# Fewer, larger groups of small attention matmuls between the large products of a fused attention and feed-forward kernel

## The chip, the cores and the metric

One core of a Trainium2 chip runs the kernel. The metric is the device time of one execution in microseconds, lower being better. The core has five engines with queues of their own that run in program order: TensorE (PE) multiplies matrices into PSUM, VectorE (DVE) and ScalarE (ACT) compute on tiles and empty PSUM, GpSimd (POOL) computes a little and issues loads, SyncE (SP) issues stores and DMA transposes. [...]

## The reference

Attention works on chunks of 64 tokens, each by itself, for 8 batches, 8 heads, 576 tokens (9 chunks) and a head dimension of 64. Its output, as 4608 rows of 512, goes through a feed-forward network with a SiLU whose slope differs for each hidden unit.

```python
scores = scale * np.matmul(q_c, k_c.transpose(0, 1, 2, 4, 3))   # per chunk of 64
scores = scores - np.max(scores, axis=-1, keepdims=True)
attn = np.exp(scores)
attn = attn / (np.sum(attn, axis=-1, keepdims=True) + 1e-09)
out = np.matmul(attn, v_c)
x = np.ascontiguousarray(out.transpose(0, 2, 1, 3)).reshape(B * S, H * D)
h = x @ w_in                                    # 4608x512 by 512x2048
g = h * (1.0 / (1.0 + np.exp(-beta * h)))
return (g @ w_out).astype(np.float32)           # 2048x512
```

## The kernel before, in words

The 4608 rows are nine blocks (NB) of 512 rows. A block is 8 chunks, taken from the flat order of batches and chunks. The whole order of instructions is written out by hand; each engine runs its own in that order. While block j goes through the feed-forward layers, the attention of block j+1 (`na`) and the scores of block j+2 are made between its matmuls.

**Attention.** `emit_T` (L136) transposes a part of q or k on DVE; a batch has four such parts, taken with `T(b)`. `emit_sc(g)` makes the scores of a group of four chunks: 64 matmuls with 32 contraction rows each (L164) into two banks, and two Exps on ACT (L173) into the tiles et. `emit_pv(i)` takes two chunks: 16 matmuls of 64 rows (L192) multiply et by v with a column of ones, so that the row sums come out beside the result. DVE takes the reciprocal of the sums (L207, or L204 when the two halves lie in separate tiles) and multiplies (L209) into x16. Then either a DMA transpose on SP's queue (L217), or in block 0 and for block 1 `emit_xp` (four PE transposes, L226, and a copy by ACT, L229), gives the block's input xt. One block needs two groups of scores and four PVs.

**First layer.** Block 0 and block 1 use plain matmuls (`L1_plain`; `emit_h` L252, SiLU by `emit_g` L262). From block 2 on, `L1` computes half of the hidden units by a scheme of seven products instead of eight: `unit` 0 and 1, whose `prod` (L305) adds into a bank A (tag sc0 or sc1) and two more, B and C (tag x). DVE copies partial results out: u1 before A is added to again, then u2, u3 and w1 (L313), and combines them to c1 (L327, L340). The other half of the hidden units is plain; three `spacers` for each unit place those matmuls between the products. The SiLUs of a unit are at L316. `emit_xs` (L285 to L288), four subtractions on DVE, makes inputs of these products from xt before the layer begins.

**Second layer.** Block 0 uses `L2_plain` (L504): 16 pieces of four matmuls, each with a hook for attention before it. Its weights are first divided by beta (`scale_w_out`: L123 on ACT, L127 on DVE). From block 1 on, `steps_L2` gives seven products mm0 to mm6 of 16 matmuls each (`prod`, L405), whose terms s1 to s4 are sums and differences of activations (`emit_sum`, L363 to L369, in four parts each). mm0 fills bank A, mm1 B, mm2 A again, mm3 D, mm4 A, mm5 C and mm6 A. ACT copies A out between (u1, u2, u3; L416), and `cB`, `cD`, `cC` combine the banks on DVE (L424). `fill` and `dve(n)` place pending s1 and s2 subtractions. The order in which a product runs through its eight parts is KO = (0, 1, 4, 5, 2, 3, 6, 7).

**Banks.** The pool ps_p has four banks for hidden units and second-layer products; ps_s has one each under the tags sc0 and sc1; ps_x has one tile of two banks, tag x. In the kernel before, scores use sc0 and sc1 and a PV uses x, except for the opening, where `spare` puts some of them in ps_p. A tile that is allocated again waits until its last reader is done.

**Around block j's second layer** the order in the queues of blocks 2 to 7 is: mm0, PV 0, mm1, PV 1, cB, mm2, PV 2, mm3, PV 3, load of the Exp table, scores of the first group, four s4 subtractions, mm4, cD, mm5, cC, scores of the second group, xs of the next block, mm6, load of the SiLU table (`table`, L653). In block 1 the scores lie a little otherwise, since the transposes of q and k come later there. Transposes for a later batch lie in the spacers 10, 13, 14 and 15 of the first layer.

Of the kernel before, what the change touches and what calls it, by code (L numbers as in the profile page):

```python
# [8 lines left out]
FP32 = mybir.dt.float32  # L9
# [6 lines left out]
def kernel(  # L16
# [103 lines left out]
    def scale_w_out(g, act=False):  # L120
        for kk in range(4 * g, 4 * g + 4):
            if act:
                nc.scalar.activation(  # L123
                    out=wo(kk), in_=wo(kk), func=ACTF.Copy,
                    scale=binv[:, kk % 2, kk // 2:kk // 2 + 1])
                continue
            nc.vector.tensor_scalar_mul(wo(kk), wo(kk), binv[:, kk % 2, kk // 2:kk // 2 + 1])  # L127
# [20 lines left out]
    def emit_sc(g, spare=False, between=None):  # L148
        sc = [
            ps_p.tile([128, 2, 4, CH], FP32, tag="p", name=f"scp{s}") if spare  # L150
            else ps_s.tile([128, 2, 4, CH], FP32, tag=f"sc{s}", name=f"sc{s}")
            for s in range(2)
        ]
        for z in range(2):
            if z and between:
                between()
            for c in range(4):
                b, cb = divmod(4 * g + c, NCB)
                for e in range(2):
                    for a in range(4):  # L160
                        p0, o0 = 32 * a, 64 * (a // 2)
                        kk = kT[b][p0:p0 + 32, z].rearrange("p t r e -> p (t r) e")
                        qq = qT[b][p0:p0 + 32, z].rearrange("p t r e -> p (t r) e")
                        nc.tensor.matmul(  # L164
                            out=sc[a % 2][o0:o0 + 64, z, c, :],
                            lhsT=kk[:, cb * CH:(cb + 1) * CH, e],
                            rhs=qq[:, cb * CH:(cb + 1) * CH, e],
                            start=(e == 0),
                            stop=(e == 1),
                        )  # L170
        for s in range(2):
            et = et_p.tile([128, 2, 4, CH], FP16, tag=f"et{s}", name=f"et{s}")
            nc.scalar.activation(out=et, in_=sc[s], func=ACTF.Exp, scale=scale)  # L173
            et_t[g, s] = et
# [5 lines left out]
    def emit_pv(i, spare=False, xbar=True):  # L180
        g = i // 2
        if spare:
            xs = [ps_p.tile([128, 4, 128], FP32, tag="p", name="xp") for _ in range(2)]
        else:
            x = ps_x.tile([128, 2, 4, 128], FP32, tag="x", name="x")
            xs = [x[:, 0], x[:, 1]]
        for s in range(4):
            z, a2 = s // 2, s % 2
            for hp, cp in ((0, 0), (1, 1), (0, 1), (1, 0)):
# [4 lines left out]
                    lhsT=et_t[g, a2][p0:p0 + 64, z, 2 * (i % 2) + cp, :],  # L194
# [193 lines left out]
    def steps_L2(j, last=False):  # L388
# [11 lines left out]
        def prod(name, a, b, first, rows=(0, 1)):  # L400
            if first and name not in bank:
                grab(name)
            for i in rows:
                for n, kk in enumerate(KO):
# [24 lines left out]
        def mm0():  # L429
            grab("B")  # L430
            prod("A", g[:, 0:NM, up], b11, True)
            take("u1", "A")
# [141 lines left out]

    with tc.manual_schedule():
# [25 lines left out]
        for f in T_items(0):  # L601
# [13 lines left out]
        emit_sc(1, spare=True)  # L615
        emit_idle(3)
        emit_pv(0, xbar=False)
        emit_pv(1, spare=True, xbar=False)
# [5 lines left out]
        emit_pv(3, spare=True, xbar=False)  # L624
# [10 lines left out]
        scale_w_out(2, act=True)  # L635
        T1[2]()
        T1[3]()
        scale_w_out(3)
# [3 lines left out]
            9: lambda: emit_sc(2),  # L642
            12: lambda: [emit_pv(4, xbar=False), emit_sc(3)],
            13: lambda: [emit_pv(5, xbar=False), emit_xp(4)],
            14: lambda: [emit_pv(6, xbar=False), emit_xp(5)],
            15: lambda: [emit_pv(7, xbar=False), emit_xp(6)],
# [5 lines left out]
        def table(func):  # L652
            nc.scalar.activation(out=warm2, in_=warm, func=func, scale=1.0)  # L653

        table(ACTF.Silu)
        TQ = {b: T_items(b) for b in range(2, B)}

        def T(b, n=1):
            for _ in range(n):
                if TQ.get(b):  # L660
                    TQ[b].pop(0)()
# [9 lines left out]
        for j in range(1, NB):  # L671
            na = j + 1
            late = j == 1
            if late:
                L1_plain(1, {
                    -1: lambda: emit_xp(7), 3: lambda: emit_tw(3), 4: lambda: T(2), 5: lambda: T(2),
# [3 lines left out]
                    KFF: lambda: [table(ACTF.Exp), emit_sc(4)],  # L680
                }, 2)
            else:
                L1(j, {8: lambda: loads(j), 10: lambda: T(j + 2), 11: lambda: loads_v(j), 13: lambda: T(j + 2),
                       14: lambda: T(j + 2), 15: lambda: T(j + 2)})

            def pv(n):
                if na < NB:
                    emit_pv(4 * na + n)

            def sc(n):  # L690
                if na + 1 < NB:
                    emit_sc(2 * na + 2 + n)
# [4 lines left out]
            emit_sum(j, 3, 3)  # L697
            if late:
                dve(8)
                T(3)  # L700
            pv(0)
            dve(4)
            mm[1]()
            if late:
                T(3)
                emit_sc(5)
            pv(1)
            cB()
            dve(2)
            mm[2]()  # L710
            pv(2)
            dve(2)
            mm[3]()
            pv(3)
            if not late:
                table(ACTF.Exp)
                sc(0)
# [4 lines left out]
            if late:  # L722
                sc(0)
# [3 lines left out]
            sc(1)  # L727
# [3 lines left out]
            table(ACTF.Silu)  # L731
# [30 lines left out]
```

## Time and profile before

| What | Value |
|---|---|
| Median of 8 runs | 282.54 us (282.29 to 283.3) |
| Profiled execution, whole | 282.52 us |
| Its span in the trace | 280.7 us |
| Granted TensorE clock | 1.0 |
| Second layer of block 0 begins on PE | 33.6 us |
| Second layer of block 1 begins on PE | 66.9 us |
| First layer of blocks 2, 3, 4 begins on PE | 83.5, 111.8, 140.1 us |
| Score matmuls, busy (x1088) | 12.5 us |
| PV matmuls into x, busy (x544) | 11.3 us |

A block in the steady part takes 28.3 us. In a timeline line the first number is the start in us from the span's start, the second the length of the merged stretch, then engine, line, operation, output and inputs, the shape and the count; in brackets stands the idle time of the engine ahead of it and who ended it. The ends of matmuls are modelled and overlap the next ones, so the distance between starts is what a matmul costs in PE's queue. Page lines on busy time give the sum, the share of the span and the number of instructions.

### The profile page before, as it was taken

To read this page: it belongs to the slowest core of one execution; us is meant where nothing else is said; L and a number is where in the kernel's file an instruction comes from. 1 tells how busy PE (TensorE), PEld (TensorE's weight loads), DVE (VectorE), ACT (ScalarE), POOL (GpSimd) and SP (SyncE) were. 2 spreads that over 40 slices of the span, in tenths; PEclk is the share of its full clock that TensorE was granted. 3 is DMA by queue.
4 is the path that set the end of the run, shared out by engine and by line. 5 is a ranking of instruction groups with operands and counts; after the bars stand their busy time and mean duration, and the time that the engine had idled before them with its cause. 6 is when DMAs were issued, how large, how long until landed. Compare 5 with 4: busy or idle time off the path is not lost.

```text
span 280.7 us, 8175 instructions
## 1 busy us (share of the span) xinstructions
PE 266.4 (95%) x3509; PEld 187.4 (67%) x3509; DVE 209.2 (75%) x395; ACT 170.7 (61%) x291; POOL 99.3 (35%) x108
## 2 busy tenths in 40 slices
PE   2679999899999999999999999999999999999995
PEld 0355445545886678667866786688668866876684
DVE  2772645897668997799778987898659865986684
ACT  2249736778247844785478547854785478527842
POOL 8743252171107710781068104810342034203400
PEclk9999999999999999999999999999999999999999
DMA  6999999999737933794479342924201420142013
GB/s 104 172 206 211 211 181 205 223 216 185 108 72 155 171 73 86 156 171 59 101 144 175 56 109 75 84 41 118 75 0 40 117 75 0 40 114 75 5 37 112
DMA packets 69588, 31.99 MB, mean 114 GB/s; under 512 B 53680, under 2 KB 63920, under 8 KB 69552
## 3 DMA queue, kind: packets, MB, share of 16 engines
q0 software_dynamic: 44960, 18.35, 54.1%
q1 hardware_dynamic: 24448, 12.99, 17.3%
q8 instruction: 27, 0.44, 0.7%
q10 hardware_dynamic: 144, 0.13, 0.1%
q14 instruction: 9, 0.07, 0.1%
HBM read 36.71 MB, written 9.44 MB: 164 GB/s over the span
## 4 chain that ended last, share of the span: by engine, by line
PE 79%; DVE 8%; ACT 5%; DMA 3%; issue 2%; POOL 2%; ACTq 0%; DVEq 0%; POOLq 0%
PE hps L252 22%; PE oA L405 18%; PE wA L305 7%; PE wX L305 6%; PE oB L405 5%; PE oD L405 5%; PE ops L504 4%; PE oC L405 4%; PE sc L164 3%; DMA vb<-in_v_dram 3%; PE x L192 3%; ACT gt L316 2%; DVE kT L136 2%; ACT L653 1%; DVE x L209 1%
## 5 line engine op out<-in xcount | busy, mean ns | idle before, releaser
L252 PE MATMUL hps<-xt,wi 128*128 128x512 f16 (+1 forms) x376 | 85.3, 365 | 1.0 <-ACT xt L229 0.9
L262 ACT ACTIVATE gt<-hps,beta 128x512 f16<-128x512 f32 x88 | 57.8, 682 | 19.4 <-PE hps L252 19.4
L252 PEld LDWEIGHTS <-wi 128*128 128x128 f16 x376 | 36.7, 98 | 30.2 <-issue 1.5
L405 PEld LDWEIGHTS <-s 128*128 128x128 f16 x496 | 46.7, 98 | 6.6 <-DVE s L369 0.5
L405 PE MATMUL oA<-tw,s 128*128 128x256 f16 x368 | 44.1, 273 | 0.0
L405 PEld LDWEIGHTS <-gt 128*128 128x128 f16 x384 | 35.7, 98 | 7.8 <-ACT gt L316 1.8
L173 ACT ACTIVATE et<-sc 128x512 f16<-128x512 f32 x34 | 18.4, 594 | 29.2 <-PE sc L164 29.2
L416 ACT COPY u<-oA 128x512 f32<-128x512 f32 x24 | 14.0, 585 | 33.9 <-PE oA L405 33.9
L313 DVE COPY u<-wA 128x512 f32<-128x512 f32 x42 | 28.6, 682 | 4.8 <-PE wA L305 4.8
L99 POOL DMA_DIRECT2D vb<-in_v_dram x32 | 27.4, 876 | 9.4 <-DMA wi<-in_moe_w_in_dram 5.5
L336 POOL TENSOR_TENSOR t<-u,w 128x512 f32<-128x512 f32 x14 | 17.8, 1273 | 34.4 <-DVE u L313 34.4
L474 POOL TENSOR_TENSOR o<-t,o 128x512 f32<-128x512 f32 x7 | 8.9, 1268 | 53.4 <-ACT o L471 53.4
L305 PEld LDWEIGHTS <-sw 128*128 128x128 f16 x224 | 21.9, 98 | 8.5
L443 POOL TENSOR_TENSOR w<-u,u 128x512 f32<-128x512 f32 x7 | 8.8, 1264 | 45.1 <-ACT u L416 45.1
L209 DVE TENSOR_TENSOR x<-x,rd 128x512 f16<-128x512 f32 x34 | 23.5, 691 | 1.2
L653 ACT ACT_TABLE_LOAD x17 | 21.8, 1283 | 4.1 <-DVE oe L485 3.8
L136 DVE STREAM_TRANSPOSE qT<-qu 128x576 f32<-128x576 f32 x16 | 19.9, 1242 | 4.5 <-DMA qu<-in_q_dram 4.5
L367 POOL TENSOR_TENSOR s<-gt 128x512 f16<-128x512 f16 x16 | 18.2, 1154 | 11.9 <-ACT gt L262 11.9
L136 DVE STREAM_TRANSPOSE kT<-ku 128x576 f32<-128x576 f32 x16 | 19.9, 1244 | 3.0 <-DMA ku<-in_k_dram 3.0
L305 PEld LDWEIGHTS <-wi 128*128 128x128 f16 x168 | 16.4, 98 | 4.9
L316 ACT ACTIVATE gt<-c,beta 128x512 f16<-128x512 f32 x28 | 18.7, 716 | 0.2
L164 PE MATMUL sc<-qT,kT 32*64 32x64 f16 x1088 | 12.5, 194 | 6.2 <-DVE kT L136 5.6
(86 smaller groups left out, 389.0 us busy)
## 6 DMA issues: line engine op xcount, KB each, us to landing
out_dram<-osb SPq DMA_DIRECT2D x21, 256.0 KB, 2.8
vb<-in_v_dram POOLq DMA_DIRECT2D x32, 144.0 KB, 7.4
qu<-in_q_dram POOLq DMA_DIRECT2D x7, 576.0 KB, 7.0
ku<-in_k_dram POOLq DMA_DIRECT2D x7, 576.0 KB, 9.1
out_dram<-o SPq DMA_DIRECT2D x14, 256.0 KB, 2.2
wi<-in_moe_w_in_dram POOLq DMA_DIRECT2D x4, 512.0 KB, 12.0
w_out<-in_moe_w_out_dram POOLq DMA_DIRECT2D x4, 512.0 KB, 16.1
qu<-in_q_dram POOLq DMA_DIRECT2D x2, 288.0 KB, 5.4
```

What stands on the lines that cost most here:

```text
L99: nc.gpsimd.dma_start(out=t[64 * hp:64 * hp + 64, 2 * z:2 * z + 2, :, 0:D].rearrange("p s c d -> p (s c) d"), in_=v[b, h0:h0 + 2].rearrang ...
L136: nc.vector.transpose(out=dst[b][:, z].rearrange("p t r e -> p (t r e)").bitcast(FP32).rearrange("p (t r) -> p r t", r=RUN), in_=src[b][:, ...
L164: nc.tensor.matmul(out=sc[a % 2][o0:o0 + 64, z, c, :], lhsT=kk[:, cb * CH:(cb + 1) * CH, e], rhs=qq[:, cb * CH:(cb + 1) * CH, e], start=(e ...
L173: nc.scalar.activation(out=et, in_=sc[s], func=ACTF.Exp, scale=scale)
L209: nc.vector.tensor_tensor(out=yy, in0=src, in1=rr.to_broadcast(shape), op=ALU.mult,)
L252: nc.tensor.matmul(out=hps_t[j, m][:, c0:c1], lhsT=w_r[m // 4][:, 2 * z + e, m // 2 % 2, m % 2, :], rhs=xt_t[j][:, n, c0:c1], start=(n == ...
L262: nc.scalar.activation(out=gt_t[j][:, m, :], in_=hps, func=ACTF.Silu, scale=beta2[:, m % 2, m // 2:m // 2 + 1],)
L305: nc.tensor.matmul(out=bank[b][:, i, :], lhsT=a[:, kk, q, i, :], rhs=rhs[:, kk, :], start=(first and i == 0 and kk == 0), stop=(kk == 1), ...
L313: nc.vector.tensor_copy(out=sb[nm], in_=bank[b])
L316: nc.scalar.activation(out=gt_t[j][:, m, cols], in_=src, func=ACTF.Silu, scale=beta2[:, m % 2, m // 2:m // 2 + 1],)
L405: nc.tensor.matmul(out=bank[name][:, i, :], lhsT=a[:, kk, i * 128:(i + 1) * 128], rhs=b[:, kk, :], start=(first and i == 0 and n == 0), st ...
L653: nc.scalar.activation(out=warm2, in_=warm, func=func, scale=1.0)
```

## The change

The attention of a block in blocks 2 to 6 stands in three places instead of five: PV 0 and 1 together after mm1, PV 2 and 3 together after mm3, and both groups of scores together after mm4. The second PV of a pair uses the banks sc0 and sc1 and is evacuated in two halves; the first group of scores uses the tile x and gets one Exp of 1024 columns instead of two of 512. et becomes one tile for both halves. All pending s1 and s2 subtractions come ahead of the first PV. In block 1, both groups of scores 4 and 5 stand ahead of mm0, and the rest as in the later blocks. Block 7 has only the PVs and block 8 has no attention.

In block 0, the second layer has the scores of groups 2 and 3 together before piece 8, PV 4 and 5 before piece 10, PV 6 and two transposed inputs before 12, PV 7 and one before 14. The last two quarters of w_out are each scaled half by ACT and half by DVE, the last quarter later than before. The Exp table is loaded before them, and the SiLU table after the last transposed input of block 1 instead of ahead of it.

mm0 runs through its parts in the order 0, 1, 4, 5, 6, 7, 2, 3. The transpose of q or k that stood in spacer 15 of the first layer comes ahead of its first product (`first`), after xs in DVE's queue. The Exp table's load moves from after mm3 and PV 3 to ahead of PV 2, and it and the SiLU table's are left out where no scores follow.

```diff
-    def scale_w_out(g, act=False):
-        for kk in range(4 * g, 4 * g + 4):
-            if act:
+    def scale_w_out(g, act=0):
+        for n, kk in enumerate(range(4 * g, 4 * g + 4)):
+            if n < act:
...
-    def emit_sc(g, spare=False, between=None):
...
+    def emit_sc(g, where="s", between=None):
+        if where == "x":
+            scx = ps_x.tile([128, 2, 2, 4, CH], FP32, tag="x", name="scx")
+            sc = [scx[:, 0], scx[:, 1]]
...
-        for s in range(2):
-            et = et_p.tile([128, 2, 4, CH], FP16, tag=f"et{s}", name=f"et{s}")
-            nc.scalar.activation(out=et, in_=sc[s], func=ACTF.Exp, scale=scale)
-            et_t[g, s] = et
+        et = et_t[g] = et_p.tile([128, 2, 2, 4, CH], FP16, tag="et", name="et")
+        for o, i_ in [(et, scx)] if where == "x" else [(et[:, s], sc[s]) for s in range(2)]:
+            nc.scalar.activation(out=o, in_=i_, func=ACTF.Exp, scale=scale)
...
+        elif where == "s":
+            xs = [ps_s.tile([128, 4, 128], FP32, tag=f"sc{h}", name="xp") for h in range(2)]
...
-            prod("A", g[:, 0:NM, up], b11, True)
+            prod("A", g[:, 0:NM, up], b11, True, order=(0, 1, 4, 5, 6, 7, 2, 3))
...
         T1[0]()
         T1[1]()
-        scale_w_out(2, act=True)
         T1[2]()
         T1[3]()
-        scale_w_out(3)
+        scale_w_out(2, act=2)
+        table(ACTF.Exp)
         load_v(2)
         load_qk(3)
         hooks = {
-            9: lambda: emit_sc(2),
-            12: lambda: [emit_pv(4, xbar=False), emit_sc(3)],
-            13: lambda: [emit_pv(5, xbar=False), emit_xp(4)],
-            14: lambda: [emit_pv(6, xbar=False), emit_xp(5)],
-            15: lambda: [emit_pv(7, xbar=False), emit_xp(6)],
+            8: lambda: [emit_sc(2, "x"), emit_sc(3)],
+            10: lambda: [emit_pv(4, xbar=False), emit_pv(5, "s", xbar=False), scale_w_out(3, act=2)],
+            12: lambda: [emit_pv(6, xbar=False), emit_xp(4), emit_xp(5)],
+            14: lambda: [emit_pv(7, xbar=False), emit_xp(6)],
         }
...
-        table(ACTF.Silu)
...
-                    -1: lambda: emit_xp(7), 3: lambda: emit_tw(3), 4: lambda: T(2), 5: lambda: T(2),
+                    -1: lambda: [emit_xp(7), table(ACTF.Silu)], 3: lambda: emit_tw(3), 4: lambda: T(2), 5: lambda: T(2),
...
-                    KFF: lambda: [table(ACTF.Exp), emit_sc(4)],
+                    KFF: lambda: [table(ACTF.Exp), emit_sc(4, "x"), emit_sc(5)],
...
-                L1(j, {8: lambda: loads(j), 10: lambda: T(j + 2), 11: lambda: loads_v(j), 13: lambda: T(j + 2),
-                       14: lambda: T(j + 2), 15: lambda: T(j + 2)})
...
+                L1(j, {8: lambda: loads(j), 10: lambda: T(j + 2), 11: lambda: loads_v(j),
+                       13: lambda: T(j + 2), 14: lambda: T(j + 2)}, first=lambda: T(j + 2))
...
             mm[0]()
             emit_sum(j, 3, 1)
             emit_sum(j, 3, 3)
+            dve(8)
             if late:
-                dve(8)
-                T(3)
-            pv(0)
-            dve(4)
+                T(3, 2)
             mm[1]()
-            if late:
-                T(3)
-                emit_sc(5)
-            pv(1)
+            pv(0, "x")
+            pv(1, "s")
             cB()
-            dve(2)
             mm[2]()
-            pv(2)
-            dve(2)
             mm[3]()
-            pv(3)
-            if not late:
+            if na + 1 < NB and not late:
                 table(ACTF.Exp)
-                sc(0)
+            pv(2, "x")
+            pv(3, "s")
             for p in range(4):
                 emit_sum(j, 4, p)
             mm[4]()
             cD()
-            if late:
-                sc(0)
+            if na + 1 < NB:
+                emit_sc(2 * na + 2, "x")
+                emit_sc(2 * na + 3)
             mm[5]()
             if j < NB - 1:
                 cC()
-            sc(1)
             if na < NB:
                 emit_xs(na)
             mm[6]()
-            table(ACTF.Silu)
+            if na + 1 < NB:
+                table(ACTF.Silu)
```

## The prediction, made before the result

> **What bounds the kernel now.** I read the page first, then the chain that ended last, then PE's timeline of one whole block beside DVE's and ACT's.
>
> ```profile
> PE 266.4 (95%) x3509; PEld 187.4 (67%) x3509; DVE 209.2 (75%) x395; ACT 170.7 (61%) x291; POOL 99.3 (35%) x108
> PE 79%; DVE 8%; ACT 5%; DMA 3%; issue 2%; POOL 2%; ACTq 0%; DVEq 0%; POOLq 0%
> ```
>
> PE is busy 95% of the span and holds 79% of the chain: it sets the end, and only what shortens or stops its queue counts. PE's timeline of block 3 (start, duration), then the oC stall in block 7:
>
> ```profile
> 124.79 2.15 PE L405 MATMUL oA<-w_out,gt 128*128 128x256 f16 x16
> 126.86 0.32 PE L192 MATMUL x<-vb,et 64*64 64x65 f16 x16
> 127.11 1.92 PE L405 MATMUL oB<-w_out,gt 128*128 128x256 f16 x16
> ...
> 129.22 1.92 PE L405 MATMUL oA<-tw,s 128*128 128x256 f16 x16
> 131.07 0.32 PE L192 MATMUL x<-vb,et 64*64 64x65 f16 x16
> 131.32 1.92 PE L405 MATMUL oD<-tw,gt 128*128 128x256 f16 x16
> 133.17 0.32 PE L192 MATMUL x<-vb,et 64*64 64x65 f16 x16
> 133.42 0.71 PE L164 MATMUL sc<-qT,kT 32*64 32x64 f16 x64
> 134.06 1.92 PE L405 MATMUL oA<-tw,s 128*128 128x256 f16 x16
> 135.82 1.91 PE L405 MATMUL oC<-w_out,s 128*128 128x256 f16 x16
> 137.66 0.71 PE L164 MATMUL sc<-qT,kT 32*64 32x64 f16 x64
> 138.30 1.92 PE L405 MATMUL oA<-tw,s 128*128 128x256 f16 x16
> ...
> 248.60 1.70 PE L405 MATMUL oC<-w_out,s 128*128 128x256 f16 x14 [0.25 <-DVE s L369]
> ```
>
> Starts, not durations, give the cost in PE's queue. A product followed by a product takes 134.06 to 135.82, 1.76; between undisturbed ones it is 1.75. Hence a PV group costs 129.22-127.11-1.75 = 0.36, PV with a score half 134.06-131.32-1.75 = 0.99, a lone score half 138.30-135.82-1.75 = 0.73. A block pays 3x0.36+0.99+0.73 = 2.80 for its five groups. Each group's time is largely the change of shape: PV's 16 starts span 0.13, and the rest is the step in (0.09) and out (0.12).
>
> The opening already has two such groups side by side:
>
> ```profile
> 12.12 0.45 PE L164 MATMUL sc<-qT,kT 32*64 32x64 f16 x32 [0.52 <-DVE bt L603]
> 12.40 0.75 PE L164 MATMUL scp<-qT,kT 32*64 32x64 f16 x64
> 15.13 0.25 PE L192 MATMUL x<-vb,et 64*64 64x65 f16 x7 [1.02 <-DMA vb<-in_v_dram]
> 15.20 0.32 PE L192 MATMUL xp<-vb,et 64*64 64x65 f16 x16
> 15.45 0.39 PE L235 MATMUL idle<-zero 128*128 128x256 f16 x2
> ```
>
> The second PV begins 0.07 after the rest of the first and is out at 15.45: 0.25 with the step out, so 0.13 joined. The joined score half is 12.40 to 13.08 less 0.12 out, 0.56.
>
> DVE where the next block's first layer begins (140.06 on PE):
>
> ```profile
> 137.84 0.69 DVE L424 TENSOR_TENSOR t<-oC,w 128x512 f32<-128x512 f32 x1 [0.51 <-PE oC L405]
> 139.57 0.42 DVE L288 TENSOR_TENSOR xs<-xt,xs 128x512 f16<-128x512 f16 x1
> 140.70 0.69 DVE L313 COPY u<-wA 128x512 f32<-128x512 f32 x1 [0.71 <-PE wA L305]
> 144.94 1.25 DVE L136 STREAM_TRANSPOSE qT<-qu 128x576 f32<-128x576 f32 x1
> 146.03 0.68 DVE L340 TENSOR_TENSOR c<-wX,u 128x512 f32<-128x512 f32 x1
> ```
>
> DVE is idle 0.71 before the copy u1; PE's third product (141.79) overwrites the bank that u1 reads, and u1 is out at 141.39: 0.40 to spare. A transpose holds DVE for 1.09 (144.94 to 146.03).
>
> **What the Trainium skill says.** TensorEngine Tiling (Array Packing), Key Properties: changing the tiling mode drains TensorE, changing only the tile does not. The trace agrees: 0.12 from a PV group to a product or to a score group, none between the two PVs at 15.20. TensorE: Matmul & The Clock Gate, Back-to-back issue gap: N/2.4+2.5 ns, 109 at 256 columns; the trace has 109. The same page, Architectural detail: ACT and DVE queues are strict FIFO; that is why an item moved ahead of u1 delays u1. ScalarE: Activation LUTs, What ACT_TABLE_LOAD costs: 1283 ns (the trace: 1283), and 186 ns + 0.833 per element without pointer operands; my estimate of the new 1024-wide Exp from this is 1.04, against 1.09 for today's pair.
>
> **The change part by part.**
>
> *Groups, blocks 2 to 6.* Two PV pairs at 0.36+0.13 and a score pair at 0.73+0.56: 0.98+1.29 = 2.27 for 2.80, so -0.53 a block. Cover: PV pair 2 needs the banks of pair 1. DVE takes a split PV in two halves of 0.55 (16.28 to 16.83), 1.09 for 0.84, +0.50 a block. From the start E of oA: all sums now stand ahead of the first evacuation; the last silu of t ends at E+1.5 (126.30), so sums end near E+5.1, evacuations at E+7.05, cB at E+7.65; pair 2 can be evacuated from about E+8.1. The score pair waits for the second half of pair 2, ready at E+10.1, wanted at E+10.5. s4 part 2 is there about 0.25 before its matmul in mm5. No wait, but thin.
>
> *Kk order of mm0.* Today the sixth matmul waits 0.22 for gt 3 (silu ends 125.50). Moved to the eighth place it doesn't wait. But mm1 follows directly now: its eighth matmul (gt 15) falls at E+2.51, and that silu ends at 127.45, E+2.66, plus 0.06. So the 0.22 goes and 0.21 comes back in oB: -0.01.
>
> *A transpose moved from the end of L1 to its front (blocks 2 to 5).* It stands between xs and u1. Let F be the end of oC's slot (137.57). DVE: t at F+0.27, four xs, the transpose at F+2.37, u1 from F+3.47 to F+4.15. In the kernel before PE's third product stood at F+4.22, since a lone score group lay in between. That group is gone from there: mm6 ends at F+1.75, the third product is due at F+1.75+1.73 = F+3.48. PE waits 0.72 with the semaphore. The later steps move with it and DVE recovers by the next spacer. +0.72 in four blocks; leaving the end of L1 wins nothing, since the silus gate the sums. Blocks 6 to 8 have no transposes left.
>
> *Block 7.* No scores: PV pairs save 4x0.36-2x0.49 = 0.46. But without a score pair mm5 comes right after mm4, while pair 2's evacuations (1.94) and the four s4 subtractions (0.33 each) follow each other on DVE. First s4 0.62 late, part 2 1.06 late, where 0.41 is lost today: +0.65. Net +0.17, with -0.02 for mm0.
>
> *Block 0, second layer.* Groups on PE's timeline, each less the 0.216 of a 512-column step: a score group 0.74, PV with scores 1.06 (44.82 to 45.79 and the step in), three PVs with PE transposes of 0.58, and a wait of 0.25 for an x16: 3.79. New: score pair 1.29, PV pair 0.49, PV with two transposes 0.80, PV with one 0.58: 3.16, so -0.63. The scaling of w_out's last quarter, halved, stays covered: ACT's two take 0.64 each behind the landing at 44.16 and are due at 46.6; DVE's two fit between evacuations, before 47.0. Then this:
>
> ```profile
> 51.17 1.28 ACT L653 ACT_TABLE_LOAD   x1
> 52.57 0.57 ACT L229 COPY xt<-xps 128x512 f16<-128x512 f16 x1
> ```
>
> PE waits 0.85 more than its own step, until 53.19, for this copy behind the table load. The load moves behind it; about 0.3 of copy latency stays: -0.55. Together -1.18: hps would resume at 52.0. The silus start 0.9 late and catch up within four banks.
>
> *Block 1.* 53.19 to 83.48 is 30.29 today. New: L1 13.05, seven products 12.23, two score pairs 2.58, two PV pairs 0.98: 28.84. -1.45. The first score pair's Exps end at 69.4 and u1's copy at 69.9, before the PVs (69.9) and mm2 (70.4): tight.
>
> *Rest.* SP still issues four transposes, but the third and fourth are back to back (1.2 each); the fourth lands about 3.3 after issue, 5.7 after pair 2 against xs at 6.0. The last table load (1.28) ran beside the last store: -0.05.
>
> Sum: -1.18-1.45+4x(0.72-0.53-0.01)-0.55+0.17-0.05 = -2.34. The profiled execution took 282.52 (span 280.7), the median is 282.54: 280.2.
>
> **Unknown costs.** The wait on u1: 0 (if DVE's queue were ahead by more than I read) to 0.9; I take 0.72. Joined PV: 0.13 to 0.36 (no join). Block 0: 0.5 to 1.4 gained. Block 1: 1.0 to 1.5. Nothing on PE can gain beyond the groups and waits named: the large matmuls keep their step of 0.109 throughout.
>
> **Rivals.**
> A, the sum: 280.2; its own range 279.4 to 281.2. Chance 0.52.
> B, the moved transpose is hidden after all: 282.54-2.34-2.88 = 277.3. For it: DVE idles 0.71 there now. Against: F+4.15 versus F+3.48. 0.15.
> C, opening and block 1 give half: waits on Exps, u1 or DMA take 1.3: 281.5. 0.13.
> D, slower: the fourth DMA transpose lands late, holding xs, the moved transpose and u1 in blocks 2 to 5. One issue of 134.78 lasted 2.11; two such back to back plus landing come to 6.8 after pair 2, 0.8 late: +3.4, 283.6. It decides for slower from 0.7 late. For it: DVE gives it later; against: most issues last 1.20. 0.13.
> E, the pairs don't join: fourteen pairs lose 0.23, 283.4. Against: 15.20. 0.07.
>
> A measurement tells 0.2% (0.57) from nothing. Faster: A, B and 0.08 of C, 0.75; same: 0.05 of C, 0.03 of D, 0.02 of E, 0.10; slower 0.15. Range 278.2 to 282.2.
>
> **What will show it.** Right: PE's third product wA in blocks 2 to 5 waits about 0.7 on DVE's u1 and not in 6 to 8; block period from 28.28 to about 28.46, block 6 at 27.56; oB waiting 0.2 on gt; oC in block 7 waiting about 1.1; hps resuming near 52.0. Wrong: an xs waiting on DMA, scores waiting on DVE, or a period under 28.0.

## The result: slower, by waits that are not in the groups

| | before | changed |
|---|---|---|
| Median of the runs compared | 282.79 us (282.29 to 284.7, 32 runs) | 289.0 us (284.54 to 290.61, 11 runs) |
| Ratio changed to before | | 1.0126 [1.0096, 1.0156] |
| Profiled execution, its span | 282.52, 280.7 | 285.13, 283.4 |

The kernel got slower, and its executions now spread over 6 us, where before all lay within 2.4 and most within 1. The ratio leaves out the executions that lie more than 1.5% above the kernel's fastest, here six of twelve (289.0 and up); they are the upper end of its own spread, so the loss between the two medians, 2.2%, is larger. The profiled execution is one of the quick ones; a later profile of the same kernel, of an execution of 288.14, stands at the end of the experiments.

The two lines of the page on busy time and on the chain that ended last:

```profile
PE 264.2 (93%) x3509; PEld 187.4 (66%) x3509; DVE 213.8 (75%) x425; ACT 163.5 (58%) x276; POOL 100.6 (36%) x108
PE 72%; DVE 11%; DMA 11%; POOL 2%; issue 2%; ACT 1%; DVEq 0%; ACTq 0%; POOLq 0%
```

PE has 2.2 us less to do (264.2 for 266.4), as it should. But the chain has left PE: 72% for 79%, while DMA went from 3% to 11% and DVE from 8% to 11%. So look for PE waiting on DVE, and DVE on a transfer.

First the groups. PE's timeline of block 2's second layer (start, length, the merged stretch):

```profile
98.62 0.32 PE L198 MATMUL x<-vb,et 64*64 64x65 f16 x16
98.77 0.30 PE L198 MATMUL xp<-vb,et 64*64 64x65 f16 x16
99.00 1.92 PE L411 MATMUL oA<-tw,s 128*128 128x256 f16 x16
100.76 1.91 PE L411 MATMUL oD<-tw,gt 128*128 128x256 f16 x16
102.60 0.32 PE L198 MATMUL x<-vb,et 64*64 64x65 f16 x16
102.75 0.30 PE L198 MATMUL xp<-vb,et 64*64 64x65 f16 x16
102.98 1.92 PE L411 MATMUL oA<-tw,s 128*128 128x256 f16 x16
104.83 0.71 PE L168 MATMUL scx<-qT,kT 32*64 32x64 f16 x64
105.36 0.86 PE L168 MATMUL sc<-qT,kT 32*64 32x64 f16 x64
106.16 1.92 PE L411 MATMUL oC<-w_out,s 128*128 128x256 f16 x16
```

By starts, oD and the second PV pair take 102.98-100.76 = 2.22; less 1.75 for a product, the pair costs 0.47. The scores take 106.16-102.98-1.75 = 1.43. Two pairs and the scores are 2.37 for the 2.80 of before. The groups save what they should within 0.1.

Then the next first layer. PE, DVE and GpSimd at the start of block 4 (three timelines of the changed kernel):

```profile
138.20 0.60 PE L311 MATMUL wA<-xt,wi 128*128 128x256 f16 x4
138.63 1.03 PE L258 MATMUL hps<-xt,wi 128*128 128x512 f16 x4
139.50 0.60 PE L311 MATMUL wX<-xt,wi 128*128 128x256 f16 x4
142.36 0.60 PE L311 MATMUL wA<-xs,sw 128*128 128x256 f16 x4 [2.26 <-DVE u L319]
```

```profile
136.72 0.69 DVE L430 TENSOR_TENSOR t<-oC,w 128x512 f32<-128x512 f32 x1 [1.25 <-PE oC L411]
137.99 0.43 DVE L291 TENSOR_TENSOR xs<-xt 128x512 f16<-128x512 f16 x1 [0.57 <-DMA xt<-x]
138.45 0.42 DVE L292 TENSOR_TENSOR xs<-xt,xs 128x512 f16<-128x512 f16 x1
138.79 0.42 DVE L293 TENSOR_TENSOR xs<-xt 128x512 f16<-128x512 f16 x1
139.12 1.49 DVE L294 TENSOR_TENSOR xs<-xt,xs 128x512 f16<-128x512 f16 x1
140.54 1.25 DVE L136 STREAM_TRANSPOSE qT<-qu 128x576 f32<-128x576 f32 x1
141.64 0.67 DVE L319 COPY u<-wA 128x512 f32<-128x512 f32 x1
```

```profile
139.06 1.27 POOL L480 TENSOR_TENSOR o<-t,o 128x512 f32<-128x512 f32 x1 [7.58 <-ACT o L477]
```

The third product (142.36) is due 1.74 after the first (138.20), at 139.93. It starts 2.43 late. Follow it back on DVE: u1 is late because the moved transpose stands before it, as forecast. But that transpose is late itself: the first xs waited 0.57 for the DMA that brings the block's input, and the fourth xs took 1.49 instead of 0.42. That one began at 139.12, 0.06 after GpSimd had begun its addition o12 at 139.06. The Trainium skill, SBUF — State Buffer, section "Who interferes with whom", says that a VectorE instruction with two SBUF inputs contends with a GpSimd instruction that reads SBUF, that the ports they share are an exclusive lock, and that the order of issue decides which of the two is held up. This trace agrees: 1.07 more for an xs that comes second.

Times of the third product's delay, read in the same way, by block (before: 0 in all). A block stands here for its first layer; the transposes that bring its input are issued during the second layer of the block before it, and "ahead" counts from the first layer's start:

| Block | 2 | 3 | 4 | 5 | 6 | 7 | 8 |
|---|---|---|---|---|---|---|---|
| delay of the third product, us | 0.68 | 0.68 | 2.43 | 0.95 | 0 | 0 | 1.93 |
| fourth DMA transpose lands, us from the first layer's start | -1.11 | -1.00 | -0.33 | -0.73 | -0.69 | -0.92 | +0.26 |
| the same before | -3.24 | -1.87 | -2.03 | -2.42 | -2.44 | -2.75 | -1.90 |

Without a late landing the first xs begins 0.87 before the first layer's start, so that 0.24 is left to spare in block 2, 0.13 in block 3, 0.05 in block 7 and nothing in the others. In the kernel before it began at -1.61 (block 8: -0.87), with 0.26 to 1.63 to spare. The fourth transpose is issued later: 4.26 ahead of the first layer in block 4, where it was 5.28. And it takes longer from issue to landing: 3.54 on average over the seven blocks, 2.81 before. All four transposes now lie close together in SP's queue; that this is the reason is shown for block 8 alone (experiment 7).

Block 7, the other loss, on PE:

```profile
248.55 0.39 PE L411 MATMUL oC<-w_out,s 128*128 128x256 f16 x2 [0.49 <-DVE s L375]
249.22 1.70 PE L411 MATMUL oC<-w_out,s 128*128 128x256 f16 x14 [0.28 <-DVE s L375]
```

By starts 0.66 and 0.44 are lost here to the s4 sums, 1.10, where before it was 0.41.

The theories for the experiments. L: the losses come from the fourth DMA transpose being late, the moved VectorE transpose adding 0.7 on top, and nothing in the groups. Rivals: the groups themselves cost more than they save (P); the moved transpose alone is the loss; the collision with GpSimd is the loss.

### The profile page after: what moved, and what is told of

Read it like the earlier page. It is cut to its first block, busy times and chain, and to the rows that moved or that the text cites. A ratio compares the mean times of both kernels' runs of the same rounds, so it can differ in the third digit from the quotient of the medians.

```text
span 283.4 us, 8191 instructions
## 1 busy us (share of the span) xinstructions
PE 264.2 (93%) x3509; PEld 187.4 (66%) x3509; DVE 213.8 (75%) x425; ACT 163.5 (58%) x276; POOL 100.6 (36%) x108
## 4 chain that ended last, share of the span: by engine, by line
PE 72%; DVE 11%; DMA 11%; POOL 2%; issue 2%; ACT 1%; DVEq 0%; ACTq 0%; POOLq 0%
PE hps L258 24%; PE oA L411 13%; PE wA L311 8%; DMA xt<-x 6%; PE wX L311 6%; PE oB L411 5%; PE oD L411 5%; PE ops L510 5%; DMA wi<-in_moe_w_in_dram 4%; DVE x L215 2%; DVE qT L136 2%; PE x L198 2%; PE oC L411 1%; POOL vb L99 1%; DVE xs L293 1%
## 5 line engine op out<-in xcount | busy, mean ns | idle before, releaser
L411 PEld LDWEIGHTS <-gt 128*128 128x128 f16 x384 | 36.5, 98 | 8.1 <-ACT gt L268 1.2
L373 POOL TENSOR_TENSOR s<-gt 128x512 f16<-128x512 f16 x16 | 19.2, 1217 | 9.0 <-ACT gt L268 9.0
L311 PE MATMUL wA<-xs,sw 128*128 128x256 f16 x112 | 16.8, 272 | 5.8 <-DVE u L319 5.8
L168 PEld LDWEIGHTS <-kT 32*64 32x64 f16 x1152 | 11.4, 106 | 10.1 <-DVE kT L136 6.4
L411 PE MATMUL oB<-w_out,gt 128*128 128x256 f16 x128 | 16.1, 273 | 0.1
```

The source lines that it names most:

```text
L311: nc.tensor.matmul(out=bank[b][:, i, :], lhsT=a[:, kk, q, i, :], rhs=rhs[:, kk, :], start=(first and i == 0 and kk == 0), stop=(kk == 1), ...
L373: tt(out=s3[:, lo], in0=g[:, lo, up], in1=g[:, lo, dn], op=ALU.subtract)
L411: nc.tensor.matmul(out=bank[name][:, i, :], lhsT=a[:, kk, i * 128:(i + 1) * 128], rhs=b[:, kk, :], start=(first and i == 0 and n == 0), st ...
```

## The experiments

**1. The transpose back behind the last lone group.** The changed kernel but for this:

```diff
-13: lambda: T(j + 2), 14: lambda: T(j + 2)}, first=lambda: T(j + 2))
+13: lambda: T(j + 2), 14: lambda: T(j + 2), 15: lambda: T(j + 2)})
```

> The changed kernel with the moved transpose of q or k put back from the front of the first layer to spacer 15; all else as changed. Theory L (two causes: the moved transpose delays u1 by 0.7 us in four blocks in every execution, and the fourth DMA transpose of a block, issued back to back with the third, now lands at about the moment when xs wants it, so that chance delays reach the critical path and are lengthened by 1.07 us when xs runs into GpSimd's o12 addition): the waits of 0.7 in blocks 2 to 5 go, 2.7 us less than the changed kernel, best times near 282, but late xs still show now and then and the times still spread by 2 us or more. Rival M (only the moved transpose costs, late landings are an accident that the kernel before has as well): best time near 280.5 and a spread under 1 us.

Measured: 281.85 (280.38 to 283.71), ratio 0.9974 [0.9951, 0.9996]; profiled 281.71. The third product is 0.10 and 0.18 late in blocks 2 and 3, and on time in 4 to 7. In block 8, which has no transpose to move, it is 1.97 late as before: there the fourth landed at +0.30 and one xs took 1.48. So in the traces the front position is about 0.7 in each of blocks 2 to 5, and block 8's delay does not depend on it. But the median fell by 7.1 (289.0 to 281.85) where 2.7 was expected; the best time, 280.38, is near what Rival M named, the spread of 3.3 is what Theory L named. One reason is in the traces: here block 3's first xs begins at -0.29, 0.58 later than -0.87, and the third product is only 0.18 late, so a late xs has 0.40 of room before PE waits. With the transpose ahead of u1 that room is gone, and a late landing counts in full. This does not account for all of the 7.1.

**2. The kernel before, with only that transpose moved to the front.**

```diff
-14: lambda: T(j + 2), 15: lambda: T(j + 2)})
+14: lambda: T(j + 2)}, first=lambda: T(j + 2))
```

> The kernel before with one part alone: the transpose of q or k moved from spacer 15 to the front of the first layer. Theory L: no cost on PE, since the lone score group between mm5 and mm6 still gives DVE 0.75 us, u1 is out at F+4.15 and the third product is due at F+4.22; 282.5 to 283.2, PE's third product waits less than 0.1 us. Rival M: the wait of 0.7 in blocks 2 to 5 is there as well, 285.3.

Measured: 282.79, ratio 1.0006 [0.9995, 1.0018]. It costs nothing here. PE and DVE of this kernel at block 4:

```profile
137.67 0.71 PE L164 MATMUL sc<-qT,kT 32*64 32x64 f16 x64
138.32 1.92 PE L405 MATMUL oA<-tw,s 128*128 128x256 f16 x16
140.07 0.60 PE L305 MATMUL wA<-xt,wi 128*128 128x256 f16 x4
...
141.81 0.60 PE L305 MATMUL wA<-xs,sw 128*128 128x256 f16 x4
```

```profile
139.92 1.25 DVE L136 STREAM_TRANSPOSE qT<-qu 128x576 f32<-128x576 f32 x1
141.01 0.68 DVE L313 COPY u<-wA 128x512 f32<-128x512 f32 x1
```

u1 is out at 141.69, and the third product starts on its time at 141.81. The lone score group at 137.67 gives PE 0.65 of other work between oC and the first layer, and so pays for the transpose. Where the change joins the scores, that cover is gone. The move and the joining each look free; together they cost 0.68.

**3. The second pair apart again.** PV 2 a product earlier:

```diff
+pv(2, "x")
 mm[3]()
...
-pv(2, "x")
 pv(3, "s")
```

> The changed kernel with the second pair of PVs taken apart: PV 2 after mm2, PV 3 after mm3, so four groups. The third DMA transpose leaves some 2 us earlier and the fourth some 0.9 us earlier. Theory L: xs is not held by a landing any more, waits at the third product stay at 0.7 in blocks 2 to 5 and are gone in 6 to 8, the split costs 0.23 us a block plus up to 0.4 of wait of PV 2 for the banks of PV 0: 283.5 to 285, spread under 1.5 us. Rival M: like the changed kernel plus 2 us or more, with the same spread.

Measured: 286.4, ratio 1.0149 [1.0111, 1.0187]. A miss: the fourth transpose was issued only 0.4 to 0.5 earlier in blocks 3 to 5 (4.7 ahead of the first layer) and 0.06 in block 2, took 3.7 to 4.1 from issue to landing in blocks 2 to 5 and landed at -0.95 to -0.60 there. The third product was late by 0.74, 1.08, 0.95 and 0.92, and by 2.50 in block 8. One half of a pair earlier is not enough: it is PV 3 that releases the fourth.

**4. o12 off GpSimd.** The addition runs on DVE behind the next block's u1:

```diff
-nc.gpsimd.tensor_tensor(out=o2, in0=sb["t"], in1=o, op=ALU.add)
-store(j, 0, 1, o2)
+def o12():
+    ...
+    nc.vector.tensor_tensor(out=o2, in0=sb["t"], in1=o, op=ALU.add)
+    store(j, 0, 1, o2)
+pend.append(o12)
...
+if m == 8:
+    pend.pop()()
 hooks.get(m, lambda: None)()
```

> The changed kernel with the last addition of a block (o12) taken from GpSimd and given to DVE behind the next block's u1, so that GpSimd reads nothing while xs runs. Theory L: no xs takes longer than 0.45 us however late it starts; the waits at PE's third product are 0.7 plus the lateness alone; best time as the changed kernel (283.5 to 285), worst under 287. Rival: the xs of 1.49 us has another cause and still occurs, the spread of the times is as before the edit.

Measured: 303.94, ratio 1.0757 [1.0738, 1.0775], where under 287 was expected. As expected, no xs is longer than 0.43 any more. But in blocks 2 to 4 the fourth transpose lands 5 us *after* the first layer's start. GpSimd's and DVE's timelines of this kernel at block 3:

```profile
109.19 0.75 POOL L89 DMA_DIRECT2D qu<-in_q_dram  x1
109.92 0.73 POOL L89 DMA_DIRECT2D ku<-in_k_dram  x1
```

```profile
121.47 0.43 DVE L291 TENSOR_TENSOR xs<-xt 128x512 f16<-128x512 f16 x1 [6.49 <-DMA xt<-x]
```

The loads of q and k (576 KB each) stand behind o12 in GpSimd's queue. In the changed kernel they are issued at 111.74, after o12, when the transposes are through (the fourth landed at 108.66). Here o12 no longer holds them, and they are issued at 109.19, while the transposes are on their way (the second at 108.41, the fourth at 112.08). Blocks 5 to 8 have no such loads at their start: there the third product is at most 0.76 late. The waits are not the whole loss: in this trace the granted TensorE clock falls to half in three stretches of 6.83 us (from 84.04, 121.59 and 155.72), each beside one of the three long waits for xt. By an estimate from these figures, half of 6.83, each costs up to 3.4.

**5. The same with a brake.** A tiny addition stands where o12 was, to keep the loads back; o12 stays on DVE:

```diff
+nc.gpsimd.tensor_tensor(out=hold, in0=sb["t"][:, :, 0:8], in1=o[:, :, 0:8], op=ALU.add)
```

> e4_o12_on_dve with one tiny GpSimd addition (128x16) put where the o12 addition was, reading the same two tiles: GpSimd's queue again waits there for ScalarE's copy of o before it issues the q and k loads. If the loads, issued 2.5 us earlier in e4_o12_on_dve, are what put the fourth transpose 5 us behind the first layer's start there, then they are issued after that start again, the fourth lands as in the changed kernel (-1.1 to +0.3), no xs is longer than 0.45, and the time is 283 to 285. If the o12 addition on VectorE itself made that kernel slow, it stays at 300 or more.

Measured: 284.22 (283.53 to 284.9), ratio 1.0041 [1.0023, 1.006]. Keeping the two loads back behind one addition of 128x16 is thus worth 20 us. GpSimd of this kernel at block 4, then DVE at block 8, first of the changed kernel and then of this one:

```profile
141.05 0.22 POOL L485 TENSOR_TENSOR hold<-t,o 128x16 f32<-128x16 f32 x1 [7.58 <-ACT o L477]
141.27 0.74 POOL L89 DMA_DIRECT2D qu<-in_q_dram  x1
```

```profile
252.89 0.42 DVE L291 TENSOR_TENSOR xs<-xt 128x512 f16<-128x512 f16 x1 [1.17 <-DMA xt<-x]
...
253.69 1.49 DVE L293 TENSOR_TENSOR xs<-xt 128x512 f16<-128x512 f16 x1
```

```profile
253.68 0.43 DVE L291 TENSOR_TENSOR xs<-xt 128x512 f16<-128x512 f16 x1 [1.22 <-DMA xt<-x]
254.14 0.42 DVE L292 TENSOR_TENSOR xs<-xt,xs 128x512 f16<-128x512 f16 x1
254.48 0.44 DVE L293 TENSOR_TENSOR xs<-xt 128x512 f16<-128x512 f16 x1
```

The fourth still lands late (block 8: +0.31), but costs 0.93 there instead of 1.93, and 1.37 in block 4 instead of 2.43. So the collision is worth 1.0 to 1.07 wherever an xs comes second, and it adds to lateness without being its source. In the medians it weighs more than in these two blocks: against the kernel before, the loss is 1.1 here (284.22 for 283.1) and was 6.2 (289.0 for 282.79), and the spread is 1.4 in five executions where it was 6.

**6. Blocks 0 and 1 alone.** From block 2 on the order of before:

```diff
+if not late:
+    ...
+    pv(0, "x"); dve(4); mm[1](); pv(1, "x"); cB(); dve(2); mm[2]()
+    pv(2, "x"); dve(2); mm[3](); pv(3, "x")
+    ...
+    emit_sc(2 * na + 2)
+    ...
+    mm[4](); cD(); mm[5](); cC(); emit_sc(2 * na + 3); emit_xs(na); mm[6]()
```

> Blocks 0 and 1 as changed, blocks 2 to 8 in the order of the kernel before (five groups, one PV step after each of four products, score halves apart, KO order, the transpose behind the last lone group). Theory L: blocks 0 and 1 keep the 2.36 that the trace of the changed kernel shows up to the start of block 2's first layer, and the rest takes what it took before: 282.8 - 2.4 = 280.4 median, every fourth transpose issued 5.2 us before the next first layer, no xs waiting on DMA. Rival (the gain of the opening is given back because block 2 then starts earlier against its loads and transposes): above 281.5, with a wait on DMA in block 2 or 3.

Measured: 281.46 (279.77 to 281.75), ratio 0.9929 [0.9902, 0.9955]; the profiled execution, 279.77, is the quickest of the six. In it block 2's first layer starts at 80.74, 2.75 earlier than before (0.29 of it already at the start of block 0's second layer, 33.33 for 33.62); every later period is as before (28.29), and no third product is late. Neither expectation holds fully: the gain is real, but the median is 1.1 above 280.4. Block 1 still has the new order, with its fourth transpose issued 4.06 ahead and landed at -0.71, the zone in which other runs lost up to 2.4; that this explains the slower executions is likely, not shown.

**7. Block 7 in the old order**, on top of experiment 1:

```diff
+if na == NB - 1:
+    pv(0, "x"); dve(4); mm[1](); pv(1, "x"); cB(); dve(2); mm[2]()
+    pv(2, "x"); dve(2); mm[3](); pv(3, "x")
+    ...
```

> The changed kernel with the transpose of the block after next back behind the last lone group (as e1_back_to_15) and, in block 7 alone, the old order of the PV steps: one each after products 1, 2, 3 and 4, all on the two-bank tile, the sums spread 4, 2 and 2. Theory L (the end is lost because the fourth DMA transpose is issued later and lands later): in block 7 the fourth is issued some 5.2 us before the next block's first layer again, the two late waits at block 8 (1.97) and about 0.3 of the oC waits go, and four PV steps cost 0.47 more than two pairs: 281.85 - 1.97 - 0.3 + 0.47 = 280.1 median, third product of block 8 not waiting. Rival P (pairs and halves cost by themselves, the transposes do not matter): no gain, 281.9 to 282.3, and block 8's third product still waits about 2.

Measured: 280.03 (277.98 to 282.58), ratio 0.9879 [0.9844, 0.9914], as Theory L has it (280.1). In block 8 the third product is on time, 1.74 after the first:

```profile
248.40 0.60 PE L311 MATMUL wA<-xt,wi 128*128 128x256 f16 x4
...
250.14 0.60 PE L311 MATMUL wA<-xs,sw 128*128 128x256 f16 x4
```

The fourth landed at -1.90, as in the kernel before. It was issued 4.32 ahead, also as before, and not the 5.2 of the forecast; what changed most is the time from issue to landing. Issued one behind each of four products, the fourth takes 2.41 here; in pairs it took 4.05, and 4.11 in experiment 1.

**8. The pairs one product earlier**, the first behind mm0 and the second behind mm2, with oB's addition behind both:

```diff
-dve(8); mm[1](); pv(0, "x"); pv(1, "s"); cB(); mm[2](); mm[3]()
-pv(2, "x"); pv(3, "s")
+dve(4); pv(0, "x"); pv(1, "s"); dve(4); mm[1](); mm[2]()
+pv(2, "x"); pv(3, "s"); mm[3]()
+...
+cB()
```

> The changed kernel with the same three groups in blocks 2 to 7, put one product earlier: first PV pair after product 1, second after product 3, the addition of oB and its store behind the second pair, sums 4 before and 4 after the first pair; the transpose of the block after next stays at the front. Theory L: the fourth DMA transpose is issued about 1.4 us earlier (5.6 before the next first layer), all xs come in time, and the third product waits 0.7 in blocks 2 to 5 (the front) and nowhere else; oB's wait of 0.2 on gt lies under the pair. From the profile of the changed kernel 285.1 - 1.75 (block 4) - 0.25 (block 5) - 1.93 (block 8) - 0.5 (block 7) - 0.95 (oB, five blocks) = 279.8. Rival P (pairs and halves cost by themselves): 284 or more, with the third product of blocks 4 and 8 still waiting about 2.

Measured: 282.84 (280.82 to 284.84), ratio 0.9996 [0.9975, 1.0017]: 3.0 above the sum. SP's timeline in block 3's second layer, of the changed kernel and of this one:

```profile
129.41 2.50 SPq L223 DMA_TRANSPOSE xt<-x  x2
132.01 0.53 SPq L387 DMA_DIRECT2D out_dram<-osb  x1
132.63 2.53 SPq L223 DMA_TRANSPOSE xt<-x  x2
```

```profile
129.43 5.99 SPq L223 DMA_TRANSPOSE xt<-x  x4
```

The last issue was at 133.94 before the first layer's start at 138.20 (4.26 ahead); here it is 5.39 ahead of 139.60. The blocks are their own control. In 3 to 7, with the fourth 5.4 to 5.5 ahead, no xs waits for more than 0.06 and the third product is late by the front's 0.68 to 0.75 in 3 to 5 and not at all in 6 and 7. In blocks 2 and 8, where it is still 4.1 ahead, it is late by 2.42 and 1.52. Theory L holds block by block; its forecast overlooked that blocks 2 and 8 do not gain those 1.2 us: block 1's order was left as it was, and the period ahead of block 8 is itself shorter, 26.35 where experiment 7 had 27.09.

**9. The same, with the transpose back behind the last lone group.**

> e7_pairs_earlier with the transpose of the block after next back behind the last lone group. Theory L: 0.7 less in each of blocks 2 to 5, 279.8 - 2.8 = 277.0, no third product waiting at all; the fastest of all kernels so far. If the front position is not what makes the third product wait 0.7 in blocks 2, 3 and 5, this takes as long as e7_pairs_earlier.

Measured: 280.56 (278.1 to 282.39), ratio 0.9899 [0.9865, 0.9933], where 277.0 was expected. DVE is busy without a gap from there into the second layer, so the transpose pushes the sums, the evacuations and the fourth DMA transpose back by 1.1: 4.2 to 4.4 ahead in blocks 3 to 6. Block 3 then lost 1.50 and block 8 1.51. The position at the front was, by accident of this saturated queue, the one that kept the transposes early.

**10. Everything early.** Experiment 8 in blocks 2 to 6, old order in block 7, block 1's pairs behind mm0 and mm1; one of the four VectorE transposes moved a block ahead, behind the addition of oD, where DVE waited 1.2 to 1.6 for oC:

```diff
+cD()
+T(j + 3)
...
-13: lambda: T(j + 2), 14: lambda: T(j + 2)}, first=lambda: T(j + 2))
+13: lambda: T(j + 2), 14: lambda: T(j + 2)})
```

> Three groups kept in blocks 1 to 6, with the fourth DMA transpose made early everywhere: in blocks 2 to 6 the pairs as in e7_pairs_earlier, in block 1 the pairs after products 1 and 2 with its two VectorE transposes behind them, in block 7 the old order of single PV steps; and of the four VectorE transposes for the block after next, the first is neither at the front nor behind the last lone group but in the second layer one block earlier, behind the addition of oD, where VectorE waited 1.2 to 1.6 us for oC. Theory L: no third product waits in any block, no xs waits on DMA, the fourth is issued 5.2 us or more before each next first layer; block 2's first layer starts at 80.7, five periods of 27.64, block 7's of 27.1, the end 28.9 after block 8's start: span 274.9, time 276.7 median (275.9 to 278), with a narrow spread. If the moved VectorE transpose holds up cC, each period is up to 0.7 longer: 280. Rival P (pairs and halves cost by themselves): 282 or more.

Measured: 279.03 (278.37 to 279.68), ratio 0.9867 [0.9847, 0.9887]. No third product is late in any block, the periods from block 2 to block 7 are 27.64 to 27.78, and four executions lie within 1.3 instead of 6. Block 1 is the miss: PE waits 0.2, 0.36, 0.36 and 0.65 there, and block 2 starts at 82.19 instead of 80.7. The first three of these waits end as ACT's Exps of groups 4 and 5 end, the second and third with the Exps that read sc0 and sc1, which the pair then writes; the last ends with nothing that the trace shows. So the expectation of the next experiment, which blames VectorE, has this in part wrong.

**11. Block 1 mended:** its pairs behind mm1 and mm2, with one VectorE transpose before the first pair and one behind the second, and oB's addition moved behind the s4 sums.

```diff
-dve(8); pv(0, "x"); pv(1, "s"); mm[1](); pv(2, "x"); pv(3, "s"); cB(); T(3, 2); mm[2]()
+dve(8); T(3); mm[1](); pv(0, "x"); pv(1, "s"); mm[2](); pv(2, "x"); pv(3, "s"); T(3)
+...
+cB()
```

> e9_slack_restored with block 1's pairs one product later (after products 2 and 3), one of its two VectorE transposes before the first pair and one behind the second, oB's addition after the s4 sums. In e9_slack_restored TensorE waited 0.2, 0.36, 0.36 and 0.65 for VectorE's x and for banks in block 1; here the gap of 1.6 on VectorE takes one transpose, and one wait of about 0.3 for a bank is left: 1.3 less, span 275.3, median 277.7 (277 to 278.4), no third product waiting. If the fourth transpose of block 1 comes late again, up to 2.4 of it is lost in block 2.

Measured: **277.28** (276.43 to 278.33), ratio **0.9795 [0.9774, 0.9815]**, the fastest of all. The profiled execution is its slowest, 278.33, and its block 2 starts at 82.15 because its block 1 began its second layer at 67.2 (66.0 in the changed kernel); what the opening lost there is not settled. PE and DVE at block 4:

```profile
137.45 0.60 PE L311 MATMUL wA<-xt,wi 128*128 128x256 f16 x4
...
139.19 0.60 PE L311 MATMUL wA<-xs,sw 128*128 128x256 f16 x4
```

```profile
134.29 1.25 DVE L136 STREAM_TRANSPOSE qT<-qu 128x576 f32<-128x576 f32 x1
135.97 0.69 DVE L430 TENSOR_TENSOR t<-oC,w 128x512 f32<-128x512 f32 x1 [0.43 <-PE oC L411]
136.58 0.41 DVE L291 TENSOR_TENSOR xs<-xt 128x512 f16<-128x512 f16 x1
```

The transpose lies in the gap ahead of t, of which 0.43 is still left, the first xs follows t without waiting for a DMA, and the third product comes 1.74 after the first. This kernel's chain that ended last:

```profile
PE 87%; DVE 4%; DMA 3%; POOL 2%; issue 1%; ACT 1%; DVEq 0%; ACTq 0%; POOLq 0%
```

PE holds 87% of it, 79% in the kernel before, while PE's busy time is 263.3 for 266.4. How much of the gain over the kernel before comes from the moved VectorE transpose alone was not tried on that kernel.

**12. The changed kernel once more,** beside number 11.

> The changed kernel as it is, once more, on the chip of e11_block1_mended. Theory L: in every execution the fourth transposes are issued at the same points and land by chance early or late; a time of 285 has two of the seven blocks with a wait over 1.5, a time of 289 needs four of them (each about 1.75 more): median 286 to 289, spread of some 4, while e11_block1_mended on the same chip spreads by less than 1.5. If the waits over 1.5 are the same two blocks in this profile and the time is 288 or more, the rest of the loss is somewhere else.

Measured: 288.9 (285.14 to 290.36), ratio 1.0176 [1.013, 1.0222]. This time the profile is of an execution of 288.14. Third products are late by 1.14, 2.57, 2.42, 0.80, 0, 0.13 and 1.93 in blocks 2 to 8, three of them over 1.5 where the expectation had four. The spread is 5.2 where some 4 was expected, and that of experiment 11 is 1.9 where under 1.5 was. Against the first profile (285.13) block 3 adds 1.89, block 2 0.46, and 0.71 went before block 2's first layer: together 3.06, where the two executions differ by 3.01. Block 3 in this profile, on DVE:

```profile
110.78 0.43 DVE L291 TENSOR_TENSOR xs<-xt 128x512 f16<-128x512 f16 x1 [0.72 <-DMA xt<-x]
...
111.91 1.49 DVE L294 TENSOR_TENSOR xs<-xt,xs 128x512 f16<-128x512 f16 x1
```

In the first profile the same block had its transpose at -1.00 and lost nothing beyond 0.68; here it landed at -0.19. The issue came at the same point, 4.24 and 4.26 ahead. So which blocks are late changes from execution to execution, and this makes part of the spread.

Another part has no profile. Of the eighteen executions of the changed kernel, ten had a mean granted TensorE clock of 0.987 to 0.994; they took 288.16 to 290.61. The other eight, both profiled ones among them, had 0.998 or more and took 284.54 to 289.46. In experiment 8 the six slowest of twenty-two (283.69 to 284.84) are just those at 0.992 to 0.994. The only trace with such a lowered clock is that of experiment 4, where it lies beside waits of 5 us. Whether the late landings bring it on here is open.

## Why the prediction was wrong, point by point

- **The groups: right, a little small.** A PV pair takes 0.47 to 0.48 for the 0.49 forecast; the step between its halves is 0.02, which agrees with the Trainium skill, TensorEngine Tiling (Array Packing), "Key Properties": a change of tiling mode drains TensorE, one of the tile alone does not. The score pair takes 1.43 for 1.29: its second half has a hold of about 0.1 that the opening's does not show. Its cause is open. Over five blocks 0.7.
- **kk order of mm0: right.** oB takes 2.04 in place of 1.84, the 0.2 that was named.
- **The transpose at the front: right for a block whose xs is on time.** Late by 0.68 in blocks 2 and 3 (0.72 forecast), by nothing in 6 and 7; experiment 2 shows that the lost score group was the cover. Not seen was that the move also uses up the 0.40 of room that a late xs would have had (experiment 1).
- **Block 7: right.** 0.66 and 0.44 lost at oC, 1.10 for 1.06.
- **Opening: right in kind, 0.7 too large.** Block 2's first layer starts 2.36 earlier, 2.63 forecast, but 0.45 of it was there before block 0's second layer began (33.17 for 33.62), where nothing is changed. From there to hps resuming (51.70) it gains 1.04 for 1.18. Block 1 then takes 29.43 for the 28.84 forecast; 0.33 of that is a wait in oD and 0.34 a hold in the scores.
- **"Rest": the step that failed.** The prediction let the fourth DMA transpose land 5.7 after pair 2, "against xs at 6.0", and priced it at nothing. Measured from the start of the second pair, the issue alone comes after 2.82 (block 3: 105.42-102.60), where the sum had about 2.4: DVE first evacuates two PVs in three pieces, and SP has a third transpose and a store ahead of it. From issue to landing it takes 3.2 to 4.05, where 3.3 was taken. It lands 6.1 (block 3) to 7.0 (block 8) after the pair, where xs are wanted at 6.2 and 5.9: a reserve of 0.1 to -1.1, where 0.3 was put down. This is the mechanism of Rival D, which had a chance of 0.13; its price counted blocks 2 to 5 and left out block 8, which lost 1.93 in both profiles.
- **What no rival had:** that a late xs also runs into GpSimd's addition. The traces of the kernels with o12 on GpSimd give the point at which it decides: with the first xs at -0.28 or earlier the fourth is still ahead of GpSimd, with -0.22 or later one xs costs 1.07 more.
- **The sum.** The profiled executions differ by +2.61 where -2.34 was forecast, 4.95 apart: third products late beyond the forecast 1.71 (block 4), 0.23 (5) and 1.93 (8), less 0.08 in 2 and 3, are 3.79; the scores 0.7; opening and block 1 0.27, the early start counted in; 0.2 is left over.
- **And the median is 3.9 above that execution.** The forecast took one time for all executions. With no reserve the landing decides anew in each, as the second profile shows for some 3 us; how much of the rest goes with the lowered clock stays open. Nor do the causes add up singly: the median falls by 7.1 without the front position, by 6.2 with the pairs earlier and by 4.8 with o12 off GpSimd and the loads held, together 18.1, where forecast and median lie 8.8 apart. So most of the loss needs several of them at once.

## What to carry to other kernels

When groups are merged, the producers inside them finish together and late: price the last product's way to its consumer (evacuation, the queue that issues it, the flight) from the trace, and compare the reserve with the spread of that flight, not with its typical value. A move that is free and a merge that is free need not be free together; test each against the cover that the other one takes away. And an engine's wait can be what keeps the DMAs behind it out of other transfers' way: before removing it, look at what it holds back.

## What was not expected of the hardware

The fourth of the four transposes takes 3.2 to 4.1 from issue to landing in the changed kernel and 2.4 to 3.35 in the kernel before. In block 4 of the first profile the packet records show one 16 KB packet of an instruction queue holding a DMA engine from 135.01 for 1.39, and packets of the hardware queue taking up to 1.47 each; a packet of that kind that came earlier in block 3, at 106.05, took 1.06 and the landing was in time. The same holds more widely: in blocks 2 to 6 of both profiles of the changed kernel, and in blocks 3 to 6 of the kernel before, the fourth lands 1.3 to 1.6 after the end of such a packet. The Trainium skill, DMA: Bandwidth & Descriptors, section "Queues, rings and completion order", says that a DMA engine takes turns between queues a whole packet at a time, which fits. That the packet makes these landings late was not tested by a run, and it does not explain block 8: there the hardware queue's packets of up to 512 bytes take at most 0.07 and the fourth still takes 4.05, and what ended that was the order of the PVs in experiment 7.
